# More warm-up products in front of the first transposes of an attention and mixture-of-experts kernel

## The chip, the cores and the metric

The kernel runs on one core of a Trainium2 chip. The metric is the device time of one execution in microseconds (us); less is better. Engines are named as the profile names them: PE is TensorE (matrix products and transposes), PEld the loading of its weights, DVE is VectorE, ACT is ScalarE, POOL is GpSimd, and SP the engine whose queue issues the transfers (DMA).

## The reference

What must be computed, cut to what matters:

```python
# attention: q, k, v of shape (2, 8, 1152, 64)
q_pool = q.reshape(B, H, S // 2, 2, D).mean(axis=3)
scores = np.matmul(q_pool, k.transpose(0, 1, 3, 2)) / np.sqrt(D)
attn = np.exp(scores - np.max(scores, axis=-1, keepdims=True))
attn = attn / (np.sum(attn, axis=-1, keepdims=True) + 1e-09)
x = np.matmul(attn, v)            # then heads side by side: (1152, 512)
# mixture of experts: w1 (4, 512, 1024), w2 (4, 1024, 512)
p = domain_probs / (domain_probs.sum(-1, keepdims=True) + 1e-09)
for e in range(4):
    out += p[:, e:e + 1] * (np.maximum(x @ w1[e], 0.0) @ w2[e])
```

## The kernel before, in words

The order on every engine is the order in which the program is written; no scheduler changes it. The attention goes through eight pairs of heads (two batches by four). Each pair has nine score tiles of 128 rows by 1152 columns. The values are float32; for the large products they are split into a high part of type fp32r and a remainder, and the parts are multiplied apart. The experts follow in a second stage, which begins some 300 us in.

Before the first pair the program issues five loads on SP (the first q rows and k, the other q rows, v). Meanwhile `make_identity` on POOL writes `ident` (float32, 128x128), DVE copies it to `identr` (fp32r), and PE transposes `ident` 14 times (`NWARM`, line 349) into a tile `warm` of the accumulator memory that nobody reads. Then pair 0 is prepared. `add_q0` (L154, DVE) adds the two q rows to be averaged. `split_k0` (L170 ACT, L171 DVE) splits k. `prep_q(0, 0)` transposes four blocks on PE (L199, tile `pq`), and `q_split` (L182 ACT, L183 DVE) splits them into `q2all`. `prep_k` transposes k in groups on PE (L225, tile `pk`) and copies them out (L232 ACT, L230 DVE). `scores(0)` multiplies on PE (L252, tile `spt`), and DVE takes the row maximum (L255, `sx`). Then come the exponentials on ACT (L261), the transposes of the probabilities on PE (L269, tile `pt`), their copies (L279 DVE, L281 ACT), and the product with v (L294, tile `po`, two halves of 64 output columns each). `spt` has one buffer, so the scores of the next tile wait until DVE has read the last.

While pair n runs, pair n+1 is prepared: its loads, `add_q` and `split_pool` on POOL (L161 to L175), `prep_q` and `prep_k` between the tiles. In the second stage `mm1` (L94) and `mm2` (L506) are long runs of fp32r products of 384 and 512 columns.

PE's tiles lie in three pools: `ps_t` (four buffers, transposes and the products of the second stage), `ps_s` (the scores) and `ps_o` (one buffer, `po`, and here `warm`).

Of the kernel before, what the change touches and what calls it, by code (L numbers as in the profile page):

```python
# [8 lines left out]
F32 = mybir.dt.float32  # L9
# [8 lines left out]
def attention_moe_kernel(ctx, tc, q, k, v, probs, w1, w2, out):  # L18
    nc = tc.nc
    B, H, S, D = q.shape  # L20
    NT, DM = out.shape
    E, _, FF = w1.shape
    P = 128
    HALF = 64
# [12 lines left out]
    ps_t = ctx.enter_context(tc.tile_pool(name="ps_t", bufs=4, space=PSUM))  # L37
    ident = const.tile([P, P], F32, name="ident")
# [18 lines left out]
    identr = const.tile([P, P], F32R, name="identr")  # L57
# [56 lines left out]
    with ExitStack() as actx:  # L114
        ap = actx.enter_context(tc.tile_pool(name="ap", bufs=1))
        ps_s = actx.enter_context(tc.tile_pool(name="ps_s", bufs=1, space=PSUM))
        ps_o = actx.enter_context(tc.tile_pool(name="ps_o", bufs=1, space=PSUM))
# [30 lines left out]
        def load_kv(dst, src, n, h0=0, h1=2):  # L148
            b, hp = pairs[n]
            nc.sync.dma_start(  # L150
                dst[:, h0:h1], src[b, 2 * hp + h0:2 * hp + h1].rearrange("h (p t) d -> p h t d", p=P))

        def add_q0(eng, t0, t1):
            eng.tensor_tensor(  # L154
                qs[:, t0:t1], qn[:, t0:t1, 0, :].unsqueeze(2).to_broadcast([P, t1 - t0, 2, D]),
                qn[:, t0:t1, 1, :].unsqueeze(2).to_broadcast([P, t1 - t0, 2, D]), ALU.add)
# [187 lines left out]
        load_kv(kn, k, 0, 1, 2)  # L344
        load_q(0, 4, 9)
        load_kv(vn[0], v, 0)
        warm = ps_o.tile([P, 320], F32, tag="o", name="warm")
        for _ in range(NWARM):
            nc.tensor.transpose(warm[:, :P], ident, ident)  # L349
        add_q0(nc.vector, 0, 4)  # L350
        split_k0(0, 0, 4)
        split_k0(0, 4, 9)
# [205 lines left out]
```

## Time and profile before

| what | value |
|---|---|
| time, median of 2 runs | 684.96 us (684.85 to 685.07) |
| the profiled execution's own time | 684.9 us |
| its span, first to last instruction | 683.1 us |
| PE busy | 670.4 us, 98% of the span |
| DVE, ACT, POOL busy | 247.1, 244.4, 201.6 us |
| mean granted TensorE clock | 0.999 |

A row of the timeline has its start, its duration, engine, line, operation, output<-input and how many instructions were merged into it. The duration of a merged row runs from the first start to the last end, so the spacing of n instructions is (duration of the row less duration of one) / (n - 1). Idle time ahead of a row stands behind it in brackets, with what ended it.

### The profile page before, as it was taken

What the parts mean: (1) busy time and instruction counts of PE and PEld (TensorE: products, weight loads), DVE (VectorE), ACT (ScalarE), POOL (GpSimd) and SP (SyncE); (2) the same over time, 40 slices, a digit from 0 to 9 for tenths busy, and PEclk for the clock granted to TensorE, in tenths of its full rate; (3) what the DMA queues carried; (4) which work ended last, traced back from release to release, by engine and by line L of the source; (5) the groups of instructions that cost most, each with busy time, mean ns of one, the idle gap of its engine ahead of it and who ended that gap; (6) DMA issues with size and microseconds to landing.
All of it is one profiled execution on the core that took longest, in us unless ns stands there. A gap on an engine that the chain in (4) does not pass through costs nothing.

```text
span 683.1 us, 9821 instructions
## 1 busy us (share of the span) xinstructions
PE 670.4 (98%) x3986; PEld 581.4 (85%) x3986; DVE 247.1 (36%) x453; ACT 244.4 (36%) x474; POOL 201.6 (30%) x242
## 2 busy tenths in 40 slices
PE   7999999999999999999999999999999999999998
PEld 6878787878787788798989898989898989898987
DVE  5656565656465655331212121212121212121211
ACT  5767676767676766321101010101020202020200
POOL 3241414141414513394260080440160530310000
PEclk9999999999999999999999999999999999999999
DMA  6735353526262650122030030020040100001011
GB/s 210 201 71 166 70 166 71 171 66 175 61 180 68 166 175 1 62 93 92 1 124 0 1 108 16 32 93 0 1 124 0 42 21 0 1 1 32 16 43 50
DMA packets 26446, 50.74 MB, mean 74 GB/s; under 512 B 2465, under 2 KB 9889, under 8 KB 26401
## 3 DMA queue, kind: packets, MB, share of 16 engines
q1 hardware_dynamic: 26400, 50.12, 25.9%
q8 instruction: 31, 0.51, 0.3%
q14 instruction: 15, 0.11, 0.0%
HBM read 30.97 MB, written 2.36 MB: 49 GB/s over the span
## 4 chain that ended last, share of the span: by engine, by line
PE 96%; DVE 2%; issue 1%; ACT 0%; POOL 0%; DVEq 0%; POOLq 0%
PE p L506 29%; PE p L94 27%; PE spt L252 13%; PE po L294 11%; PE pt L269 9%; PE p1t L94 3%; DVE sx L255 2%; PE pk L225 2%; PE pr L317 2%; PE pq L199 1%; PE warm L349 0%; DVE k L230 0%; ACT sx L261 0%; ACT q2all L182 0%; ACT aT L281 0%
## 5 line engine op out<-in xcount | busy, mean ns | idle before, releaser
L94 PE MATMUL p<-xh,wslot 128*128 128x384 f32 x640 | 166.7, 339 | 0.0
L255 DVE TENSOR_SCALAR_CACHE_REDUCE sx<-spt 128x1152 f32<-128x1152 f32 x72 | 97.7, 1357 | 71.5 <-PE spt L252 70.0
L94 PEld LDWEIGHTS p<-xh,wslot 128*128 128x128 f32 x640 | 116.7, 188 | 0.4
L94 PE MATMUL p<-xl,wslot 128*128 128x384 f32 x320 | 108.3, 338 | 0.0
L261 ACT ACTIVATE sx<-sx,mn 128x1152 f32<-128x1152 f32 x72 | 90.7, 1259 | 14.2 <-DVE sx L255 14.1
L252 PE MATMUL spt<-k,q2all 128*128 128x384 f32 x384 | 84.7, 355 | 8.0 <-DVE sx L255 6.2
L281 ACT ACTIVATE aT<-pt 128x384 f32<-128x384 f32 x144 | 70.7, 491 | 55.4 <-PE pt L269 52.2
L252 PEld LDWEIGHTS spt<-k,q2all 128*128 128x128 f32 x384 | 64.3, 188 | 28.0 <-DVE sx L255 13.2
L269 PE MATMUL pt<-ident,sx 128*128 128x128 f32 x648 | 82.5, 272 | 0.0
L96 ACT ACTIVATE hb<-p 128x384 fp32r<-128x384 f32 x48 | 23.6, 492 | 159.9 <-PE p L94 158.3
L294 PE MATMUL po<-aT,vn 128*64 128x320 f32 (+1 forms) x576 | 77.6, 410 | 0.0
L269 PEld LDWEIGHTS pt<-ident,sx 128*128 128x128 f32 x648 | 75.1, 141 | 2.7 <-issue 0.4
L506 PE MATMUL p<-wslot,hb 128*128 128x512 f32 (+1 forms) x348 | 75.8, 375 | 0.0
L506 PEld LDWEIGHTS p<-wslot,hb 128*128 128x128 f32 x348 | 62.2, 188 | 11.6
L511 DVE SCALAR_TENSOR_TENSOR acc<-p,pw,acc 128x512 f32<-128x512 f32 (+1 forms) x28 | 20.5, 731 | 124.1 <-PE p L506 124.1
L294 PEld LDWEIGHTS po<-aT,vn 128*64 128x64 f32 x576 | 39.3, 137 | 28.3 <-issue 3.4
L96 ACT ACTIVATE k<-p 128x384 fp32r<-128x384 f32 x30 | 14.8, 492 | 130.6 <-PE p L94 130.6
L94 PEld LDWEIGHTS p<-xl,wslot 128*128 128x128 f32 x320 | 60.0, 188 | 0.4
L306 POOL TENSOR_TENSOR dg<-ident,rs 128x256 f32<-128x256 f32 x32 | 19.0, 615 | 128.6 <-DVE rs L304 128.6
L97 DVE SCALAR_TENSOR_TENSOR hb<-p,hb 128x384 fp32r<-128x384 f32 x48 | 26.8, 558 | 76.6 <-ACT hb L96 76.6
L100 POOL TENSOR_SCALAR wslot<-stg 128x512 fp32r<-128x512 f32 x12 | 7.5, 622 | 157.0 <-PE p L94 79.4
L506 PE MATMUL p<-wslot,k 128*128 128x512 f32 x168 | 51.9, 390 | 0.0
(103 smaller groups left out, 759.1 us busy)
## 6 DMA issues: line engine op xcount, KB each, us to landing
kab<-k SPq DMA_DIRECT2D x32, 288.0 KB, 4.8
q2all<-q2all SPq DMA_DIRECT2D x28, 256.0 KB, 4.7
vn<-in_v_dram SPq DMA_DIRECT2D x8, 576.0 KB, 6.8
kn<-in_moe_w_dram SPq DMA_DIRECT2D x8, 512.0 KB, 3.4
qn<-in_moe_w_dram SPq DMA_DIRECT2D x8, 512.0 KB, 3.4
stg<-in_moe_w_dram SPq DMA_DIRECT2D x8, 512.0 KB, 3.4
qs<-in_moe_w_dram SPq DMA_DIRECT2D x8, 512.0 KB, 3.4
qn<-in_q_dram SPq DMA_DIRECT2D x7, 576.0 KB, 6.2
```

The costliest lines, as they stand in the source:

```text
L94: nc.tensor.matmul(pt, w[:, a, kt, fs], x[:, kt, cols], start=(j == 0), stop=(j == last))
L96: nc.scalar.activation(hh[ft], pt, AF.Relu)
L97: nc.vector.scalar_tensor_tensor(hl[ft], pt, 0.0, hh[ft].bitcast(F32), ALU.max, ALU.subtract)
L252: nc.tensor.matmul(spt[g][:, c, :NC], w, x, start=(j == 0), stop=(j == len(ops) - 1))
L255: nc.vector.tensor_scalar(sx[g % NX].rearrange("p (c x) -> p c x", c=3), spt.pop(g)[:, :, :NC], -INV, None, ALU.mult, ALU.min, accum_out=m ...
L261: nc.scalar.activation(sx[g % NX], sx[g % NX], AF.Exp, bias=mn[g % NX], scale=-1.0, accum_out=sums[n % 2][:, i:i + 1])
L269: nc.tensor.transpose(pt[:, j, :], sx[g % NX][:, kt * P:(kt + 1) * P], ident)
L281: nc.scalar.activation(dst, src, AF.Copy)
L294: nc.tensor.matmul(po[h * HALF:(h + 1) * HALF, :w], vn[n % 2][:, h, kt, :], aT[grp][:, h, kt, :], start=(kt == 0), stop=(kt == KT - 1))
L306: nc.gpsimd.tensor_tensor(dg[:, h, :256].rearrange("p (j q) -> p j q", j=2), ident.unsqueeze(1).to_broadcast([P, 2, P]), r[:, h:4:2].unsqu ...
L506: nc.tensor.matmul(pc, h[ft][:, ts_], where[e, 2, ft // 4][:, a, ft % 4, c0:c1], start=(m == 0), stop=(m == len(ops) - 1))
L511: nc.vector.scalar_tensor_tensor(ac, pc, pw[:, tt, e:e + 1], ac, ALU.mult, ALU.add)
```

## The change

The warm-up tile becomes four tiles of the pool `ps_t`, and behind the 14 transposes, still ahead of `prep_q(0, 0)`, PE gets 72 more products that nobody reads: 8 of fp32r with all 128 rows and 512 columns (`identr` against itself four times over), 16 such on half of the rows each (64 rows, alternating halves, each half into a tile of its own), 16 more on all rows, and 32 float32 transposes on half of the rows each, of 64 columns. Nothing else changes.

```diff
-        warm = ps_o.tile([P, 320], F32, tag="o", name="warm")
+        warm = [ps_t.tile([P, 512], F32, tag="t", name="warm") for _ in range(4)]
         for _ in range(NWARM):
-            nc.tensor.transpose(warm[:, :P], ident, ident)
+            nc.tensor.transpose(warm[0][:, :P], ident, ident)
+        halves = [slice(0, HALF), slice(HALF, P)]
+        wide = identr.unsqueeze(1).to_broadcast([P, 4, P])
+        for _ in range(8):
+            nc.tensor.matmul(warm[0], identr, wide, start=True, stop=True)
+        for _ in range(8):
+            for a, r in enumerate(halves):
+                nc.tensor.matmul(warm[2 + a], identr[r, :], wide[r], start=True, stop=True)
+        for _ in range(8):
+            for a in range(2):
+                nc.tensor.matmul(warm[a], identr, wide, start=True, stop=True)
+        for _ in range(16):
+            for a, r in enumerate(halves):
+                nc.tensor.transpose(warm[2 + a][:, :HALF], ident[r, :], ident[r, r])
         add_q0(nc.vector, 0, 4)
```

On PE the program begins so before (the names in brackets are the engines whose semaphores an instruction waits for):

```order
L349 MATMUL warm<-ident 128x128 [waits Pool_49]
L349 MATMUL warm<-ident 128x128 x13
L199 MATMUL pq<-ident,qs 128x128 [waits DVE_49]
L199 MATMUL pq<-ident,qs 128x128 x3
L225 MATMUL pk<-identr,khl 128x128 [waits DVE_49]
L225 MATMUL pk<-identr,khl 128x128 x3
```

The same place of the changed program:

```order
L349 MATMUL warm<-ident 128x128 [waits Pool_49]
L349 MATMUL warm<-ident 128x128 x13
L353 MATMUL warm<-identr 128x512 [waits DVE_49]
L353 MATMUL warm<-identr 128x512 x7
L356 MATMUL warm<-identr 128x512 x16
L359 MATMUL warm<-identr 128x512 x16
L362 MATMUL warm<-ident 128x64 x32
L199 MATMUL pq<-ident,qs 128x128 [waits DVE_49,PE_49]
L199 MATMUL pq<-ident,qs 128x128 x3
L225 MATMUL pk<-identr,khl 128x128 [waits DVE_49,PE_49]
L225 MATMUL pk<-identr,khl 128x128 x3
```

The four lines of new products stand between the old transposes and `pq`; `pq` and `pk` now also wait for PE's own earlier writes, since they take over the buffers of `warm`. The other engines keep their order.

## Rows read from the trace of the kernel before

**Rows 1.** The page: busy time of each engine, and the granted TensorE clock in 40 equal slices.

```profile
PE 670.4 (98%) x3986; PEld 581.4 (85%) x3986; DVE 247.1 (36%) x453; ACT 244.4 (36%) x474; POOL 201.6 (30%) x242
...
PEclk9999999999999999999999999999999999999999
```

**Rows 2.** The chain of work that ended last, in order of time, in the first 30 us: start, us, what.

```profile
1.35 3.25 PE warm L349 x14
4.60 0.87 PE pq L199 x4
...
5.49 0.61 ACT q2all L182
...
7.46 0.97 PE spt L252 x4
```

**Rows 3.** The timeline of the opening: warm-up, preparation of q and k, and the first scores.

```profile
1.33 0.27 DVE L58 CAST identr<-ident 128x128 fp32r<-128x128 f32 x1 [1.33 <-POOL ident masks.py:199]
1.35 3.25 PE L349 MATMUL warm<-ident 128*128 128x128 f32 x14 [1.35 <-POOL ident masks.py:199]
3.44 0.69 DVE L154 TENSOR_TENSOR qs<-qn 128x512 f32<-128x512 f32 x1 [1.85 <-DMA qn<-in_q_dram]
4.39 1.06 PE L199 MATMUL pq<-ident,qs 128*128 128x128 f32 x4
5.10 1.35 PE L225 MATMUL pk<-identr,khl 128*128 128x128 f32 x9
5.49 0.60 ACT L182 ACTIVATE q2all<-pq 128x512 fp32r<-128x512 f32 x1 [0.56 <-PE pq L199]
6.62 0.68 PE L252 MATMUL spt<-k,q2all 128*128 128x384 f32 x2 [0.17 <-ACT k L232]
```

**Rows 4.** The timeline, the same operations later: `pq` and `pk` again, and the transposes of a tile.

```profile
8.28 0.94 PE L225 MATMUL pk<-identr,khl 128*128 128x128 f32 x9
11.64 0.60 PE L199 MATMUL pq<-ident,qs 128*128 128x128 f32 x4
150.75 1.15 PE L269 MATMUL pt<-ident,sx 128*128 128x128 f32 x9
```

**Rows 5.** The instructions of the tiles `warm`, `ident`, `identr` and `spt` by line: count, duration in ns (least/median/most), first and last start in us.

```profile
L349 PE MATMUL warm<-ident x14: 421/421/475, 1.3 to 4.2; 128*128 128x128 f32 x14
L269 PE MATMUL pt<-ident,sx x648: 270/272/331, 14.5 to 280.6; 128*128 128x128 f32 x162
L225 PE MATMUL pk<-identr,khl x144: 226/252/455, 5.1 to 234.4; 128*128 128x128 f32 x144
L252 PE MATMUL spt<-k,q2all x384: 331/337/446, 6.6 to 268.7; 128*128 128x384 f32 x192
```

**Rows 6.** The timeline of PE at the start of an `mm2`: fp32r products of 512 columns on all rows, back to back.

```profile
513.42 0.63 PE L506 MATMUL p<-wslot,k 128*128 128x512 f32 x2
513.88 0.39 PE L506 MATMUL p<-wslot,khl 128*128 128x512 f32 x1
514.11 0.63 PE L506 MATMUL p<-wslot,k 128*128 128x512 f32 x2
514.58 0.39 PE L506 MATMUL p<-wslot,khl 128*128 128x512 f32 x1
514.80 0.63 PE L506 MATMUL p<-wslot,k 128*128 128x512 f32 x2
```

**Rows 7.** The timeline of PE around a product with v, whose instructions take turns on two halves of the columns.

```profile
155.26 2.32 PE L294 MATMUL po<-aT,vn 128*64 128x320 f32 x16
157.51 1.33 PE L252 MATMUL spt<-k,q2all 128*128 128x384 f32 x6
```

**Rows 8.** Busy time by stretches of 4 us: stretch, length, PE, PEld, DVE, ACT, POOL busy (instructions), granted clock, share of the DMA engines, GB/s.

```profile
4.00:8.00 4.00, 3.67 (x21) 3.19 (x20) 2.87 (x6) 2.63 (x6) 0.52 (x1) 1.00 0.76 269
8.00:12.00 4.00, 2.73 (x22) 2.40 (x20) 2.26 (x5) 2.04 (x4) 1.55 (x1) 1.00 0.38 111
12.00:16.00 4.00, 2.65 (x19) 2.14 (x17) 3.19 (x6) 3.17 (x7) 1.70 (x2) 1.00 1.00 288
16.00:20.00 4.00, 3.92 (x26) 3.62 (x27) 2.73 (x6) 3.54 (x7) 3.20 (x4) 1.00 1.01 220
20.00:24.00 4.00, 2.43 (x18) 2.16 (x17) 2.43 (x4) 2.77 (x7) 0.96 (x1) 1.00 1.02 339
24.00:28.00 4.00, 4.00 (x37) 3.72 (x36) 3.59 (x5) 3.45 (x8) 0.00 (x0) 1.00 1.03 245
```

**Rows 9.** Who waited for whom in the first 20 us, the rows of PE: us in total, times, longest.

```profile
PE spt L252 <- DVE k L230: 1.4, 2, 1.3
PE spt L252 <- DVE sx L255: 1.4, 2, 1.0
PE warm L349 <- POOL ident masks.py:199: 1.3, 1, 1.3
...
PE spt L252 <- ACT k L232: 0.2, 1, 0.2
```

**Rows 10.** The timeline: the last POOL step that prepares k of pair 1, and the first PE transposes that read it.

```profile
19.54 1.42 POOL L175 TENSOR_TENSOR khl<-kn,khl 128x576 fp32r<-128x576 f32 x1
...
24.76 0.89 PE L225 MATMUL pk<-identr,khl 128*128 128x128 f32 x8
```

## The prediction

> **What bounds the kernel now.** First the page: PE is busy for 98% of the span, the three other engines for about a third [rows 1]. So almost any time put into PE's queue ahead of useful work comes out at the end, unless the place where it is put has idle time of its own. The place is the opening, so I read the chain of waits there: from 1.35 us the chain is the 14 warm-up transposes, then `pq`, then the splitting of q on ACT, then scores [rows 2]. The warm-up is thus already on the path, not beside it: `qs` is complete at 3.44 + 0.69 = 4.13 us, but `pq` starts at 4.39, which is where the 14 transposes have been issued [rows 3]. PE's queue holds `pq` back by 0.26 us even before anything is added.
>
> Then the spacing, which tells PE's speed. The 14 transposes take 3.25 us, one of them 0.42 [rows 3, 5]: (3.25 - 0.42) / 13 = 0.217 us apart. Nine later ones of the same size are (1.15 - 0.27) / 8 = 0.109 us apart [rows 4, 5]. That is the factor between the clock's two levels, 1.2 and 2.4 GHz, although the column of granted clock already reads 1.00 there [rows 8]. The four of `pq` still take 1.06 us at 4.39 and only 0.60 us at 11.64 [rows 3, 4]; the nine of `pk` 1.35 against 0.94. The first two scores at 6.62 stand 0.68 - 0.44 = 0.24 us apart [rows 3, 5], between the levels. So the rise falls at about 6.7 us, and after it nothing stays slow. This bounds any gain from a better warm-up: 0.46 us on `pq`, 0.41 on `pk`, about a tenth on the scores, one microsecond in all.
>
> **The change, part by part.** It removes nothing and adds 72 products ahead of `pq`. Their input `identr` is ready at 1.33 + 0.27 = 1.60 us [rows 3], so they start at 4.39, right behind the 14.
>
> *Wide products on all rows, 24.* Nearest rows: fp32r products of 512 columns in `mm2`, where three take from 513.42 to 514.11, 0.23 us each [rows 6]. At the low level I take twice that, 0.46. From 4.39 to 6.7 five of them fit (2.31 us). The other 19 take 19 x 0.23 = 4.37 us.
>
> *Wide products on half the rows, 16.* No row shows half rows. Upper bound: each like a full one, 16 x 0.23 = 3.68 us. Lower bound: the two halves side by side, 8 x 0.23 = 1.84 us. The nearest row is the product with v, which alternates halves of the columns: 16 of 320 columns in 157.51 - 155.26 = 2.25 us, 0.14 us each [rows 7]. A float32 transpose of 128 columns needs 0.109 us; at that rate per column 320 would need 0.27 us, so two halves share their time. I take side by side, 1.84 us.
>
> *Float32 transposes on half the rows, 32 of 64 columns.* Upper bound: like the full ones, 32 x 0.109 = 3.5 us. Lower bound: half the columns and side by side, 32 x 0.027 = 0.87 us. Weights must be loaded for each, and the closest instructions of any product with 128 columns of weights are those of `pk`: (0.94 - 0.25) / 8 = 0.085 us [rows 4, 5]. I take that, 2.7 us.
>
> *Changes between whole and half rows, 4.* The product with v also leaves whole-array use, and the scores behind it start at 157.51, before its modelled end of 157.58 [rows 7]: no gap is seen. I take 0. The upper bound is one emptied pipeline each, 0.39 - 0.23 = 0.16 us [rows 6], 0.64 us in all. The Trainium skill ("TensorEngine Tiling (Array Packing)", Key Properties) says that changing the tiling mode drains TensorE; by that the upper bound would hold, and the time below would be 0.6 us more. The trace, which shows changes of column halves only, does not show such a drain.
>
> *The new waits of `pq` and `pk` on PE itself.* They are for writes issued earlier on the same queue; the longest, of `pk`'s third and fourth groups, are behind transposes issued just before `pq`, and four of `pq` lie between. Nothing queues behind them that is not delayed already: 0, at most one result latency of 0.27 us [rows 5].
>
> Sum: `pq` starts at 6.7 + 4.37 + 1.84 + 2.7 = 15.6 us instead of 4.39, 11.2 us later. By then the clock is high, and `pq` ends 1.06 - 0.60 = 0.46 us sooner after its start; the ACT and DVE steps behind it keep their lengths. Net 10.8 us on the first scores.
>
> *What of it is hidden.* PE's idle time between 4 and 24 us is 0.33 + 1.27 + 1.35 + 0.08 + 1.57 = 4.6 us [rows 8], and it would shrink if it waited for something that does not move. In the table of waits, apart from the start, PE waits only for DVE's and ACT's steps on `k` and `sx` [rows 9], and those read what PE wrote. They move with PE. The transfers are dense from 12 to 28 us (share about 1.0 [rows 8]), but what they bring is early: k of pair 1 is split by 19.54 + 1.42 = 20.96 us and first read at 24.76 [rows 10]. Later, PE has next to no idle time. So nothing is taken off: the profiled execution's 684.9 us (the median is 684.96, no difference) become 684.9 + 10.8 = 695.7.
>
> **The rivals.**
> 1. *Half rows one after the other.* The half-row products then cost 3.68 and the transposes up to 3.5 us: 2.6 us more, with drains 3.3, so 698 to 699. For it: no row shows row halves sharing the array. Against: column halves do share it.
> 2. *The clock stays at 1.2 GHz longer.* Each microsecond at the low level costs half of it. Were all 72 slow, they would take 24 x 0.46 + 8 x 0.46 + 32 x 0.17 = 20.2 us, and the 0.46 would not come back: 705.1. It passes 2% (13.7 us) if the rise comes some 6 us later than 6.7. Against it: the rise came in a stretch in which PE had run nothing but transposes, and the added products are denser. The Trainium skill ("TensorE: Matmul & The Clock Gate", Part 4) says that transpose-mode work does not count as PE-busy for the clock; by that the 14 transposes would do nothing, and the rise would come somewhere between 9.7 us (as long after the first wide product as it came after the first transpose: 3.0 us later, 697.2) and the end of the wide products (24 x 0.46 + 8 x 0.46 + 2.7 - 0.46 = 17.0 us, 701.9). This trace disagrees: transposes alone preceded its rise.
> 3. *Part is absorbed.* If all 4.6 us of idle time closed while DVE, ACT and the transfers ran ahead, 691.1. For it: the loads of q for pair 1 do not depend on PE. Against: rows 9, as above.
> 4. *Not slower.* The opening would have to be set by the transfers and POOL, so that the delay disappears in front of the first `pk` of pair 1. For that its input would have to be ready no earlier than 24.76 + 10.8 = 35.6 us; it is ready at 20.96 [rows 10], 14.6 us too early, and its k load itself starts only when pair 0's k has been split. Likewise if products that nobody reads were not run; but the 14 of before are run [rows 5]. Time 684.9. A pure gain from the clock cannot pay either: at most one microsecond stands against 10.8.
>
> **How the numbers follow.** Forecast 0.69, rival 1 0.12, rival 2 0.09, rival 3 0.07, rival 4 0.03. The likeliest case gives 695.7. Its own range: down 1.85 us if the half transposes are at their lower bound, and 1.15 more if the clock rises with the first wide products, 692.7; up 0.8 for the transposes and 0.64 for drains, 697.1. The range stretches up over rival 1: 692.8 to 699.0. Below it lie rivals 3 and 4, above it most of rival 2: about 0.18 outside. What a measurement of this kernel can tell from no change, taken as 2%, is 13.7 us, that is 698.7 us and up: half of rival 2 and a third of rival 1, 0.09. Faster by 2% has no case, 0.01. Within 2%: 0.90.
>
> **What would show it.** In the changed profile `pq` should start at about 15.6 us and take 0.60 us. The 8 first wide products should be 0.46 us apart up to about 6.7 us and 0.23 after. The half-row pairs should be 0.23 us apart as pairs (0.46 says rival 1), the half transposes 0.085 each. The distance from the start of `pq` to the first scores should shrink by about half a microsecond, and the idle time of PE after it should keep its pattern, shifted. From 30 us on every PE row should stand about 10.8 us later and end so. The prediction is wrong if PE's idle time behind `pq` falls by microseconds (rival 3), or if the added stretch is under 8 or over 14 us long.

## The result, and the profile after

The changed kernel takes 694.73 us (median of 2 executions, 694.06 and 695.41) against 684.96: a ratio of 1.0143, 95% interval 1.0099 to 1.0186. It is slower by 9.8 us, inside the forecast range of 692.8 to 699.0 and 1.0 us below the forecast 695.7. By 2% it counts as the same. The profiled execution is the longer one, 695.41 us.

The page after, first lines: span, and busy time of each engine (before: [rows 1]).

```profile
span 693.6 us, 9968 instructions
...
PE 681.1 (98%) x4058; PEld 589.3 (85%) x4058; DVE 247.1 (36%) x453; ACT 244.4 (35%) x474; POOL 201.1 (29%) x242
```

PE has 72 instructions and 10.7 us of busy time more; the span grew by 10.5 us. DVE and ACT did the same work. The timeline of PE in the opening shows where it lies (before: [rows 3, 4]):

```profile
1.34 3.25 PE L349 MATMUL warm<-ident 128*128 128x128 f32 x14 [1.34 <-POOL ident masks.py:199]
4.25 3.18 PE L353 MATMUL warm<-identr 128*128 128x512 f32 x8
7.35 2.11 PE L356 MATMUL warm<-identr 64*128 64x512 f32 x16
9.39 3.94 PE L359 MATMUL warm<-identr 128*128 128x512 f32 x16
13.26 1.22 PE L362 MATMUL warm<-ident 64*128 64x64 f32 x32
14.41 0.66 PE L199 MATMUL pq<-ident,qs 128*128 128x128 f32 x4
14.83 0.97 PE L225 MATMUL pk<-identr,khl 128*128 128x128 f32 x9
16.25 0.68 PE L252 MATMUL spt<-k,q2all 128*128 128x384 f32 x2 [0.45 <-ACT k L232]
17.09 0.96 PE L252 MATMUL spt<-k,q2all 128*128 128x384 f32 x4 [0.15 <-DVE k L230]
17.89 0.92 PE L225 MATMUL pk<-identr,khl 128*128 128x128 f32 x9
20.11 2.20 PE L252 MATMUL spt<-k,q2all 128*128 128x384 f32 x6 [1.30 <-DVE k L230]
22.11 1.06 PE L199 MATMUL pq<-ident,qs 128*128 128x128 f32 x4
23.77 1.31 PE L252 MATMUL spt<-k,q2all 128*128 128x384 f32 x6 [0.60 <-DVE sx L255]
```

From start to start the four new groups take 3.10, 2.04, 3.87 and 1.15 us. `pq` starts at 14.41 instead of 4.39, the first scores at 16.25 instead of 6.62: 9.6 us later. The waits behind stay where they were and as long (1.30 us before the second tile's scores, 1.27 before). Then comes a row that the prediction did not have: at 20.11 six scores take 2.20 us instead of 1.3, and the four of `pq` 1.06 instead of 0.60. Busy time by stretches (columns as in [rows 8], granted clock behind the POOL column):

```profile
16.00:20.00 4.00, 2.41 (x15) 1.84 (x15) 3.64 (x6) 2.17 (x6) 0.44 (x1) 1.00 0.23 56
20.00:21.00 1.00, 0.89 (x3) 0.89 (x4) 0.06 (x1) 0.84 (x2) 0.00 (x0) 0.62 0.95 336
21.00:23.00 2.00, 2.00 (x9) 1.66 (x7) 0.65 (x1) 0.00 (x0) 0.39 (x1) 0.50 1.10 266
23.00:24.00 1.00, 0.40 (x2) 0.23 (x2) 0.88 (x3) 0.80 (x2) 0.92 (x3) 0.68 1.02 217
```

The granted clock is at 0.50, that is 1.2 GHz, from 20.2 to 23.6 us, behind four microseconds in which PE was busy for 2.41. That adds 0.9 us, and 9.6 becomes the 10.5 of the span. The other execution, 694.06 us, has a span of 692.3 and a mean clock of 0.999 against 0.997.

### The profile page after: what moved, and what is told of

It is laid out like the page before. It is cut to its first block, busy times and chain, and to the rows that moved or that the text cites. A ratio compares the mean times of both kernels' runs of the same rounds, so it can differ in the third digit from the quotient of the medians.

```text
span 693.6 us, 9968 instructions
## 1 busy us (share of the span) xinstructions
PE 681.1 (98%) x4058; PEld 589.3 (85%) x4058; DVE 247.1 (36%) x453; ACT 244.4 (35%) x474; POOL 201.1 (29%) x242
## 4 chain that ended last, share of the span: by engine, by line
PE 96%; DVE 2%; issue 1%; ACT 0%; POOL 0%; DVEq 0%; POOLq 0%
PE p L519 28%; PE p L94 27%; PE spt L252 13%; PE po L294 11%; PE pt L269 9%; PE p1t L94 2%; DVE sx L255 2%; PE pk L225 2%; PE pr L317 2%; PE warm L359 1%; PE warm L349 0%; PE pq L199 0%; PE warm L353 0%; PE warm L356 0%; DVE k L230 0%
## 5 line engine op out<-in xcount | busy, mean ns | idle before, releaser
L96 ACT ACTIVATE hb<-p 128x384 fp32r<-128x384 f32 x48 | 23.6, 492 | 159.9 <-PE p L94 159.9
L96 ACT ACTIVATE k<-p 128x384 fp32r<-128x384 f32 x30 | 14.8, 492 | 130.6 <-PE p L94 130.6
```

Source lines behind the costliest of these rows:

```text
L96: nc.scalar.activation(hh[ft], pt, AF.Relu)
```

## The experiments

**The changed kernel again** (no edit).

> The changed kernel as it is, more often, to see what its executions share. The first profile has a stretch from 20.1 to 22.7 us at a granted clock of 0.57 (mean clock 0.997, span 693.6 us); the other execution has a mean clock of 0.999 and a span of 692.3. Theory A (the fall at 20 us is chance, and the change costs the 9.6 us by which the first scores are later): most executions have clock 0.999 and a span of about 692.5, time 694.2, and those with a clock of 0.997 are about 1.3 us longer. Theory B (the fall belongs to the change): it is in most executions, and all are near 695.4.

Measured: 694.02, 694.46, 694.47 and 694.89 us (ratio 1.0129, interval 1.0105 to 1.0152). A fifth execution took 1576 us and is left out: its granted clock fell to 0.16 at 503 us and stayed there. Theory A holds for these four: the clocks are 0.999 to 1.000, so none has the fall at 20 us, and it need not go with the change. But the kernel before, timed beside it, was not one group: nine executions had 684.65 to 685.32 us, one 686.00, and five 687.8 to 688.95 at a mean clock of 0.992 to 0.995.

**Without the half transposes.**

```diff
-        for _ in range(16):
-            for a, r in enumerate(halves):
-                nc.tensor.transpose(warm[2 + a][:, :HALF], ident[r, :], ident[r, r])
```

> The 32 float32 transposes on half rows are left out. They take 13.26 to 14.41 us in the changed kernel's trace. If PE's queue carries every added microsecond to the end: 1.15 us less than the changed kernel, about 693.0 without a fall of the clock, and pq starts at 13.3. Rival (part of the added time is hidden by work that runs ahead): less than 0.5 us of difference.

Measured: median 693.30, 1.17 us less than the 694.47 beside it. The four executions of each kernel do not overlap but spread over 0.7 and 0.9 us, so the agreement with 1.15 is closer than the data allow. The traces say it better: `pq` starts at 13.22, and the span less this start is 691.6 - 13.22 = 678.4 us, against 683.1 - 4.39 = 678.7 in the kernel before. PE's queue carries the added time to the end. No sign of the rival.

**Half-row products, one half after the other.**

```diff
-        for _ in range(8):
-            for a, r in enumerate(halves):
+        for a, r in enumerate(halves):
+            for _ in range(8):
                 nc.tensor.matmul(warm[2 + a], identr[r, :], wide[r], start=True, stop=True)
```

> The same 16 half-row products, but the 8 of the first half before the 8 of the second. If halves share the array only when they follow each other in turn: 16 x 0.23 = 3.7 us instead of 2.04 for this group, and the time 1.7 us above the changed kernel (about 695.9 without a fall of the clock). If a half-row product is simply faster, in any order: no difference, 694.2.

Measured: 695.40 us, 0.9 above the changed kernel. Neither number came. The timeline of PE in this kernel:

```profile
7.40 3.17 PE L356 MATMUL warm<-identr 64*128 64x512 f32 x16
10.50 3.96 PE L359 MATMUL warm<-identr 128*128 128x512 f32 x16
```

The group takes 3.10 us instead of 2.04, not 3.7. Halves do share the array, and the order matters, but not only neighbours overlap: seven products start and end between 8.43 and 9.50 us, where products 0.23 us apart with 0.39 us each would be four.

**Only the new tiles.** The 72 products are left out; `warm` stays in the pool of the transposes.

> Only the four warm-up tiles in the pool of the transposes, none of the 72 products. If the new tiles and the waits on PE that come with them cost nothing: 685.0, as before. If pq or pk wait there for PE's own writes: up to 0.3 us more.

Measured: ratio 1.0004 (0.9982 to 1.0025); that interval is wider than the 0.3 us in question, but the trace settles it. The profiled execution took 685.15 us, its `pq` starts at 4.38 and its first scores at 6.62, as before. The tiles and the waits on PE cost nothing. The kernel also has longer executions, 3 of 10 at 687.35 to 688.67.

**Six wide products in place of the 14 transposes.**

```diff
-        for _ in range(NWARM):
-            nc.tensor.transpose(warm[:, :P], ident, ident)
+        for _ in range(6):
+            nc.tensor.matmul(warm, identr, wide, start=True, stop=True)
```

> Six fp32r products of 512 columns on all rows instead of the 14 transposes, and nothing else: they can start when identr is ready at 1.60 us, take 6 x 0.43 = 2.6 us at the low clock and end about when qs is ready (4.13), so pq starts at 4.2 instead of 4.39. If the clock's rise stays at 6.7 us: 684.7, against 684.9 before. If wide products bring the rise sooner: up to 0.9 less, 684.0. On the executions of before that are 1 to 4 us longer at a mean clock of 0.992 to 0.997 (6 of 15): if they come from a thin warm-up, this kernel has fewer of them; if they are chance, about as many.

Measured: ratio 0.9981 (0.9963 to 1.0000). The best executions equal those of before (684.64 against 684.61). In the trace `pq` starts at 4.38, not at 4.2, and the first scores at 6.55 instead of 6.62, so the opening gains 0.07 us at most. The gain, which the interval only just allows, would lie in the longer executions: 1 of 12 above 686.5 us, against 10 of 23 of before beside it.

**No warm-up.** The 14 transposes are left out too.

> All warm-up taken out, the 14 transposes too. pq can start at 4.13, 0.26 us sooner. If the warm-up buys nothing: 684.7. If the 14 transposes bring the clock's rise forward: the rise comes after 6.7 us, the scores of tile 0 and what follows run at half speed for some microseconds, and the time is 685 to 688, with a mean clock no higher than 0.995.

Measured: ratio 1.0001 (0.9979 to 1.0023), which settles nothing against a before in two groups. The best execution, 685.42 us, is 0.8 above the best of before, and seven of ten lie above 686.5, against 10 of 23. The mean clocks are 0.994 to 1.000, not all below 0.995. In its trace `pq` starts at 4.33, not 4.13, although PE has nothing ahead of it: the sum of q is complete at 4.19. The scores at 11.70 take 2.29 us, and the clock is low from 11.4 to 14.8. This fall does not speak for the warm-up, since the trace also has the collision of two steps that is described below (L171 takes 2.14 us).

**The same delay from transposes alone.**

```diff
-        for _ in range(NWARM):
+        for _ in range(NWARM + 81):
```

> Before, with 95 instead of 14 identity transposes and no wide product: about the delay of the change in another currency. 11 more up to 6.7 us, then 70 at 0.109 us: pq starts at 14.3. If only the length of the added stretch counts: 694.4, as the changed kernel. If transposes do not keep the clock as the wide products do: a fall of the clock in the stretch or soon after it, mean clock 0.992 to 0.997, and 1 to 4 us more.

Measured: 693.29 to 693.46 us in four executions, 696.20 in the profiled one; ratio 1.0095 (1.0062 to 1.0127), overlapping the changed kernel's. In the time no difference between the kinds of product is seen. In the trace `pq` takes 0.60 us at 14.33, although PE had run nothing but transposes: the clock was at its higher level. Then it fell, and the longer time is that; one of five executions here and one of the 12 of the changed kernel in all runs are too few to tell them apart:

```profile
20.00:21.00 1.00, 1.00 (x4) 1.00 (x5) 0.00 (x0) 0.70 (x2) 0.00 (x0) 0.64 1.05 394
21.00:27.00 6.00, 5.39 (x21) 4.80 (x20) 3.25 (x4) 2.67 (x6) 4.13 (x5) 0.50 1.04 221
27.00:28.00 1.00, 1.00 (x9) 1.00 (x8) 0.95 (x5) 0.53 (x2) 0.46 (x1) 0.94 0.97 267
```

**Before again, for a trace of a longer execution** (no edit).

> Before, unchanged, for another trace. In 15 executions beside the first four experiments it had 685.1 us at clock 1.000 or 0.999 nine times and 686.0 to 689.0 at 0.992 to 0.999 six times. If such a longer one is caught: the low granted clock should lie in the sparse opening between 8 and 24 us, and the lengthening should be there too, 3 us at a clock of 0.992. Otherwise 685.1 and a clock of 1.00 throughout.

It caught one: 688.2 us, clock 0.992. The clock is at 0.50 from 9.4 to 19.6 us, as expected:

```profile
9.00:10.00 1.00, 0.63 (x6) 0.66 (x6) 1.00 (x2) 0.00 (x0) 0.00 (x0) 0.70 0.52 101
10.00:14.00 4.00, 3.54 (x16) 3.15 (x14) 1.62 (x4) 2.00 (x4) 1.54 (x2) 0.50 0.94 277
14.00:18.00 4.00, 3.39 (x13) 3.01 (x12) 2.31 (x4) 2.33 (x5) 0.69 (x2) 0.50 1.04 213
18.00:20.00 2.00, 2.00 (x11) 2.00 (x10) 1.50 (x5) 1.14 (x3) 1.92 (x3) 0.59 1.01 207
```

But something comes ahead of the fall. The timeline of this execution, POOL, DVE and PE:

```profile
7.05 1.56 POOL L154 TENSOR_TENSOR qs<-qn 128x640 f32<-128x640 f32 x1 [4.83 <-DMA qn<-in_q_dram]
...
7.54 1.68 DVE L171 TENSOR_TENSOR khl<-kn,khl 128x576 fp32r<-128x576 f32 x1
...
9.37 1.33 PE L225 MATMUL pk<-identr,khl 128*128 128x128 f32 x9 [0.94 <-DVE khl L171]
```

and the same two steps in the first profile of before, 685 us:

```profile
7.37 0.76 DVE L171 TENSOR_TENSOR khl<-kn,khl 128x576 fp32r<-128x576 f32 x1
...
7.48 2.08 POOL L154 TENSOR_TENSOR qs<-qn 128x640 f32<-128x640 f32 x1 [5.25 <-DMA qn<-in_q_dram]
```

Whichever of the two starts first runs at its own length (POOL 1.56, DVE 0.76 us); the other is held until it ends: DVE to 9.22, which is 0.61 after POOL's 8.61, POOL to 9.56, which is 1.43 after DVE's 8.13. Between the two traces q landed 0.43 us apart, and L171 moved by 0.17 the other way; that is enough to change who is first. If POOL is first, the second `pk` is 1.1 us late (9.37 against 8.28). The Trainium skill ("SBUF — State Buffer", section "SBUF: two separate sides") has this rule: a DVE operation with two inputs in SBUF and a GpSimd operation that reads SBUF take an exclusive lock on a shared pair of ports, and the later one blocks entirely. The two traces agree. In the changed kernel's traces the two do not meet: POOL's L154 runs at 7.23 and DVE's L171 waits behind `pq` until 16.97.

```profile
16.97 0.76 DVE L171 TENSOR_TENSOR khl<-kn,khl 128x576 fp32r<-128x576 f32 x1
```

Seven traces have both steps so close together. DVE is first in three (before, only the new tiles, six wide products), and the clock does not fall in them. POOL is first in four (this one, no warm-up, and the two kernels that follow), and it falls in all four.

**Wide products in PE's later waits**, with the six wide products in front, and with the 14 transposes in front.

```diff
         for c in range(3, 6):
             prep_k(0, c)
+        for _ in range(4):
+            nc.tensor.matmul(warm, identr, wide, start=True, stop=True)
...
         prep_q(0, 1)
+        for _ in range(3):
+            nc.tensor.matmul(warm, identr, wide, start=True, stop=True)
         exps(1)
```

> The six wide products in the free time before pq, and seven more of the same kind in PE's later waits of the opening: four behind the second pk (a wait of 1.3 us, 4 x 0.23 = 0.9) and three behind the second pq (a wait of 1.0 us, 3 x 0.23 = 0.7). They lie in idle time and cost nothing by themselves. Theory (the granted clock falls in the opening because PE is too little busy there): no execution above 685.5, median 684.9. Rival (the falls have another cause, or come from a wait elsewhere): about as many executions above 686 as with the six products alone (3 of 12).

> Before with its 14 transposes, and only the seven wide products in the two later waits. By the theory that PE's sparse work from 7 to 16 us lets the clock fall: the executions of 687 to 689 us (9 of 24 beside the last experiments) go away, median 685.0. If the fall is decided earlier, by the warm-up itself: as many as before.

Measured: ratios 0.9988 (0.9972 to 1.0005) and 0.9985 (0.9968 to 1.0002); 12 executions each, none above 687.4 us, where 9 of the 23 of before beside them were. But 3 and 2 of them lie between 686.8 and 687.4, so the expectation of none above 685.5 fell. Both traces are of such executions: POOL was first (L171 takes 1.93 and 2.09 us), the clock falls (at 9.4 and 9.9 us) as in before's longer execution, and the products follow when it has fallen. There they are not free: k of the second group is ready at 11.2 and 11.4 us, and the scores that read it start behind the products, at 12.41 and 12.57. In the kernel with six wide products in front:

```profile
9.00:10.00 1.00, 0.57 (x5) 0.61 (x5) 1.00 (x2) 0.00 (x0) 0.00 (x0) 0.69 0.38 83
10.00:12.00 2.00, 2.00 (x11) 1.71 (x10) 1.16 (x3) 1.31 (x3) 0.00 (x0) 0.50 0.94 285
12.00:13.00 1.00, 1.00 (x5) 0.90 (x4) 0.00 (x0) 0.69 (x2) 0.07 (x1) 0.61 0.98 293
13.00:14.00 1.00, 1.00 (x9) 0.97 (x8) 0.15 (x1) 0.00 (x0) 1.00 (x1) 1.00 1.04 277
```

The clock is back at 12.8 us, in the other kernel at 13.3, where it was at 19.6 in before's traced execution. That fits the missing executions above 687.4. It does not show that the products brought the clock back: without any, the low stretch lasted 10.2 us there, 6.8 with 95 transposes, and 3.4, as long as here, in the changed kernel and in the one without warm-up.

**The changed kernel once more.**

> The changed kernel once more beside these two, since only four comparable executions of it lay beside before so far. If the wide warm-up keeps most of the clock's falls away: times within 694.0 to 695.5, no group 3 us higher as before has. If the falls are as frequent as before: a third of the executions at 697 to 698.

Measured: 693.38 to 694.30 us in six executions, ratio 1.0102 (1.0081 to 1.0124). No higher group, and the lower end is under the expected 694.0. The ratio is below the first on both sides: before had a median of 685.86 us here, with 11 of 23 above 686.5, and the changed kernel's median is 693.61. In this trace the eight wide products take 2.16 us from start to start instead of 3.10: the clock rose about two microseconds sooner, and `pq` starts at 13.46.

```profile
4.25 2.23 PE L353 MATMUL warm<-identr 128*128 128x512 f32 x8
6.41 2.12 PE L356 MATMUL warm<-identr 64*128 64x512 f32 x16
```

**The adding of q on DVE.**

```diff
-        add_q0(nc.gpsimd, 4, 9)
...
         for c in range(3, 6):
             prep_k(0, c)
+        add_q0(nc.vector, 4, 9)
```

> Before with its 14 transposes and no new product; only the adding of q rows 4 to 9 (L154) moves from POOL to DVE, behind DVE's copy of the second pk. Theory C: the longer executions of before (686 to 689 us) begin where POOL's L154 starts ahead of DVE's L171 (7.05 against 7.54 us in the trace of such an execution); L171 then takes 1.7 us instead of 0.76, the second pk is 1.1 us late, and the granted clock falls at 9.3 us. With the two steps apart L171 should take 0.76 us always, and the times should be one group, 684.5 to 685.5, with the 14 transposes as they are. Rival (the clock falls by chance or for want of warm-up, and the late pk only goes with it): a third or more of the executions stay at 686.8 to 689. Own cost: DVE is idle from 10.4 to 11.8 us, the step takes about 0.86, and the next load of q starts some 1.7 us later, which should not reach PE.

Measured: ten of 12 executions at 685.01 to 685.43 us, two at 686.36 and 687.13; before beside it had 4 of 16 at 686.6 to 688.5. Ratio 0.9993 (0.9980 to 1.0006). The trace is of the longest execution. L171 takes 0.76 us in it, `pk` starts at 8.74, and yet the clock falls, at 11.1 us, until 17.9:

```profile
7.83 0.76 DVE L171 TENSOR_TENSOR khl<-kn,khl 128x576 fp32r<-128x576 f32 x1 [0.91 <-ACT khl L170]
...
13.81 2.29 PE L252 MATMUL spt<-k,q2all 128*128 128x384 f32 x6 [0.60 <-DVE sx L255]
```

So the theory does not hold as it was put: the clock can fall without the collision. Neither does the rival, which wanted a third of the executions at 686.8 to 689 and got one. The seven traces above tie the collision to the fall, but this test does not show it as the cause: 2 longer of 12 against 4 of 16 is too few to tell, and none at 688 against two beside it likewise.

## Why the prediction came out right

**The mechanism.** It was that `pq` is queue-bound from 4.39 us on, so that everything put ahead of it moves the end. That is what happened: 9.6 us at the first scores, no less at the end, and the group of 1.15 us that was taken out alone gave its time back. One reading under it was off: the queue was said to hold `pq` back by 0.26 us already in the kernel before. Without any warm-up `pq` starts at 4.33, so it was about 0.1.

**The terms.** The eight first wide products: 4.39 to 7.39 by the sum, 4.25 to 7.35 measured, with the rise at about the forecast time in that execution. That time was luck. It was read from the first two scores of before, which take 0.68 us; they take 0.68 at 16.25 in the changed kernel too, where the clock is high. In the trace of before the ninth `pk` already has the later length (0.25 us at 6.21), and among the traces with the same 14 transposes the rise lies anywhere from ahead of 4.5 us to about 7. The range allowed for a sooner rise, with 1.15 us. Single starts of the other groups (each row with x2 is a pair, one product on either half):

```profile
7.03 0.40 PE L353 MATMUL warm<-identr 128*128 128x512 f32 x1
7.35 0.50 PE L356 MATMUL warm<-identr 64*128 64x512 f32 x2
7.69 0.40 PE L356 MATMUL warm<-identr 64*128 64x512 f32 x2
...
9.07 0.39 PE L356 MATMUL warm<-identr 64*128 64x512 f32 x2
9.39 0.50 PE L359 MATMUL warm<-identr 128*128 128x512 f32 x1
9.72 0.40 PE L359 MATMUL warm<-identr 128*128 128x512 f32 x1
...
12.94 0.39 PE L359 MATMUL warm<-identr 128*128 128x512 f32 x1
13.26 0.28 PE L362 MATMUL warm<-ident 64*128 64x64 f32 x2
```

The pairs stand (9.07 - 7.69) / 6 = 0.23 us apart, as forecast (8 of them, 1.84 us), and so do the full products behind (12.94 - 9.72) / 14 = 0.23 (16 of them, 3.68). Rival 1 is out. What the groups take beyond that, 0.2 us each, lies at the changes between whole and half rows.

**Two terms were wrong, in opposite directions.** The first is that of the 32 half transposes: 2.7 us by the spacing of `pk`. The group takes 1.15; its 16 pairs stand 0.06 us apart, 1.0 in all, and the rest is the change to them. I took the row with 128 columns of weights as the nearest and so let the weights set the pace. The rows of the changed kernel show the loads of weights overlapping:

```profile
L362 PEld LDWEIGHTS warm<-ident x32: 135/139/142, 13.3 to 14.2; 64*128 64x128 f32 x32
L362 PE MATMUL warm<-ident x32: 221/223/274, 13.3 to 14.3; 64*128 64x64 f32 x32
```

Each load lasts 0.139 us while a pair starts every 0.06. The lower bound, half the columns and side by side (0.87 us), was the nearer one.

The second is that of the four changes, taken as 0. Across the first, two steps take 7.69 - 7.03 = 0.66 us instead of 0.46; across the second, 9.72 - 9.07 = 0.65. Each costs 0.2 us, and the two around the half transposes some 0.15 each: 0.7 in all, about the upper bound of 0.64 and not 0. The row it was read from changes column halves only. The Trainium skill says ("TensorEngine Tiling (Array Packing)", Key Properties) that a change of mode drains TensorE; these rows agree.

Together, from 7.26 us, where a ninth wide product would have started: 7.26 + 1.84 + 3.68 + 1.0 + 0.6 = 14.4, the measured start of `pq` (the last change falls in part behind it), 1.2 us earlier than forecast.

**The luck in the number.** The sum was 1.7 us too long for the transposes and 0.6 too short for the changes, and the fall of the clock in the profiled execution, which the sum did not have, added 0.9 there. The 11 executions of the changed kernel without that fall have a mean of 694.0 us, 1.7 below the forecast 695.7.

**The saving.** Forecast 0.46 us between `pq` and the first scores; 2.23 became 1.84, 0.39; the four of `pq` take 0.66 us and not 0.60, since their first stands behind the last change.

**Rival 2, the clock.** A long low stretch at the start did not occur. The Trainium skill's rule ("TensorE: Matmul & The Clock Gate", Part 4) that transposes do not count as PE-busy, by which 697 to 702 us were possible, fails here for float32 transposes: behind 95 of them and nothing else, `pq` took 0.60 us and not 1.06. A short low stretch did occur, but later and in one of 12 executions, where it cost 0.9 us. No step of the prediction had it.

**Rivals 3 and 4.** Nothing was absorbed within an execution. But the prediction took before as one number. Of the 77 comparable executions of before that were timed beside the experiments 30 lie above 686.5 us, and their mean is 686.3; the 12 of the changed kernel lie between 693.4 and 695.4, with a mean of 694.1. Against the 685 that both profile and sum started from, the change costs 9 us; against the mean, 7.8. The difference is the longer executions of before, which the changed kernel hardly has. The delay takes L154 and L171 apart, and in the traces the fall of the clock goes with their collision; but it also came without one, so that the collision makes up the difference is argued and not shown.

## What to carry to other kernels

A warm-up may be as long as the wait that it fills, here until 4.33 us, and no longer: behind that every product on this queue was paid in full. What it could win is less than the microsecond of the prediction: in the trace with the adding of q on DVE the clock was high by `pq` (0.64 us at 4.33), and the first scores came at 6.44 instead of 6.62. If a kernel's executions fall into groups, look at what two engines do at the same time just ahead of the first difference; a step of 0.76 us that takes 1.7 says more than the mean clock. Products in idle waits cost nothing only while they fit: at the low clock they held the scores up by 1.1 and 1.2 us. They did not prevent a fall of the clock here, and that they shorten it is likely (none of 24 executions above 687.4 us, against 9 of 23) but not shown. Six wide products in free time, or seven in the waits, may beat before by 0.15 to 0.2%; the intervals (0.9963 to 1.0000, 0.9968 to 1.0002) do not settle it. Both were timed with the collision left in; the version with these products and the adding of q on DVE was not tried.

## What the runs showed of the hardware that was not expected

- Products on the two halves of the rows share the array: 16 of 512 columns in 2.04 us in turn, in 3.10 when one half was written behind the other, where 16 on all rows take 3.87. A change between whole and half rows costs 0.15 to 0.2 us.
- The granted clock fell to 0.50 in the opening of some executions and not in others of the same kernel. What decides it stays open: PE was busy for 2.41 of 4 us ahead of the fall in the changed kernel's first profile, and for 2.41 in the same stretch of its last one (15 to 19 us, since its rows stand 0.95 us earlier), where no fall came.
- POOL and DVE held each other up, in either order, over the adding of q and the splitting of k: 0.76 us became 1.68, or 1.56 became 2.08.
